# A two-level Strassen MLP on one core: product 6 of the second matmul also gets an inner level

## The chip, the cores and the metric

One core of a Trainium2 chip runs the kernel. The metric is the device time of one execution in microseconds (us); of a kernel that was run several times, the median is given. The engines of the core are TensorE (PE in the profile; its weight loads are PEld), VectorE (DVE), ScalarE (ACT), GpSimd (POOL) and SyncE (SP), which issues nearly all transfers.

## The reference

`x` is 1 x 2048 x 1024, `w1` 1024 x 3584, `w2` 3584 x 1024, all bf16.

```python
def reference(x, w1, b1, w2, b2):
    y = _layernorm(x, axis=-1)
    h = _gelu(jnp.einsum("bsd,df->bsf", y, w1) + b1)
    return jnp.einsum("bsf,fd->bsd", h, w2) + b2
```

## The kernel before

**Blocks.** The 2048 rows are two blocks (`s` = 0 and 1) of 1024. Each block runs matmul 1 (`y` times `w1`, then gelu into `h_sb`) and matmul 2 (`h` times `w2`). Both use Strassen's scheme in Winograd's form: an operand is cut into 2 x 2 quarters, seven products of quarter sums replace eight, and sums of the products give the four result quarters. The sums of operands are made by VectorE; those of `w2` are made once, in block 0, and kept in DRAM (`w2_sums`; in the code `tq`, with T1 to T4).

**Matmul 1 of block 1** runs in seven chunks of two units each; a chunk takes 28 x 2 matmuls of 512 columns on L608. Of product `P` in unit `u` the kernel keeps a copy `sn` (L621, ScalarE or VectorE), VectorE adds a later product to it (`c7`, `c3`, L626), and ScalarE applies gelu (L632). The next product in the same PSUM bank waits for the copy or the sum: P4 of a unit waits for its `c7`, P6 for the copy of P1, P7 for the copy of P6.

**Matmul 2** has seven products of 512 x 512 with a depth of 14 x 128. In block 1 they run in the order 1, 5, 2, 6, 7, 3, 4 (`SEQ2`). A product is run in one of two ways:

- `plain` (L797): four tiles, each of 14 matmuls of 512 columns; one operand is a whole quarter of `w2` (1792 KB).
- `inner` (L864): one more Winograd level. Seven sub-products, in the order 1, 5, 6, 2, 7, 3, 4, each of 14 matmuls of 256 columns. VectorE makes four sums of the `h` operand (`iS5`, `iS6`, `iS7`, `iS3`, each of 1792 16-bit columns, L681). Each sub-product has its own piece of `w2` of 448 KB: three raw, four sums that lie in DRAM (`w2_inner_sums`, `ti`). Sums of the sub-products follow on VectorE (L761) and ScalarE (L781): here called `k1`, `k2`, `k5` (intermediate), `o11`, `o12`, `o21`, `o22` (the four results) and `s2` (a copy into a bank that is accumulated upon).

`INNER` lists which products are `inner`; in block 1 all but product 6.

**Sums over products in block 1** (U and V style, in f32 tiles `sn_sb`): g1 is product 1, g5 product 5. Product 6 was accumulated by TensorE on top of g1: ScalarE first copies g1's four tiles into four banks (`seed`), the plain product is run on them, ScalarE copies the result out (`V`), and VectorE adds g5 (`O12`, four operations of 512 columns). Product 7 accumulates on V, product 3 on O12; `o22` adds g5 to product 7's result in four operations of 512 columns and is stored.

**The inner sums of w2.** Block 0 stores those of products 1 to 4 (`is`). For products 5 and 7 `t_inner` (L1130 and on) makes them during matmul 1 of block 1: SP loads one quarter from `w2_sums` into `x_sb` (`tl`, 1792 KB), VectorE makes four sums (`tI`, 1792 columns, L1138), and SP stores each (`ts`, 448 KB). The buffers are used in turn, so the load for product 7 waits until all four stores of product 5 have landed.

**What sets the order.** A planner (`Planner.place`) orders all operations of an engine before the kernel is built, by costs, due times and free buffers that are written into the code. Each engine then runs its list strictly in that order (`_emit`), with semaphore waits. So an operation that waits holds back everything behind it in its engine's list; SP's list of transfers is such a list too. TensorE has 8 PSUM banks; `sn_sb` has 12 tiles.

**Weights in block 1 of matmul 2** lie in 22 buffers of 448 KB (`A0`.. to `X1`); `hold` names, product by product, the buffers of its seven pieces. `fetch` issues their loads, each waiting for the sub-product that last read the buffer. Product 6, being plain, took the four buffers `A` at once (`load_w2`).

Of the kernel before, what the change touches and what calls it, by code (L numbers as in the profile page):

```python
# [29 lines left out]
N_WARM = 26  # L30
OPEN_JOBS = 5
SEQ2 = ((5, 1, 2, 6, 7, 3, 4), (1, 5, 2, 6, 7, 3, 4))
INNER = ((1, 2, 3, 4), (1, 5, 2, 7, 3, 4))
LN_ACT = (2, 4, 6)
DMA_T = (4, 6)

# [200 lines left out]
def bass_standalone__mixer_channel_mlp__prompt_kernel(  # L237
# [24 lines left out]
    with ExitStack() as es:  # L262
# [487 lines left out]
        def mm2_block(s, W):  # L750
# [6 lines left out]
            A = {q: (h[q], [[h_ok[(s, q, u)]] for u in range(NU)]) for q in h}  # L757
            users = {p: [] for p in SEQ2[s]}
            stores = []
            done = lambda p: users[p]  # L760
            plus = lambda e, out, x, y: e.tensor_tensor(out=out, in0=x, in1=y, op=ALU.add)  # L761

# [72 lines left out]
                users[p] += flat(t1, t2, t3, t4)  # L835
                return {1: Y["11"], 2: Y["21"], 3: Y["22"], 4: t4, 5: t1, 6: t2, 7: t3}

            def inner(p, a, Yo, xb, war, O=None, bias=None, out=None, gate=(), kk=None):

# [55 lines left out]

                g, ok = O
                ho = [Holder(outs, 2), Holder(outs, 2)] if out is not None else [None, None]
                hk = Holder(snaps) if kk is None else None  # L900

                def kk_q():
                    t = kk if hk is None else sn_sb[:, hk.k, :]
                    return t.rearrange("p (v c) -> p v c", v=2)

                def o_q(i, j):
                    return quart(g, i, j) if out is None else o_sb[:, ho[i].k:ho[i].k + 2, j * HI:(j + 1) * HI]

                sd = copy(lambda: bank_q(c2), lambda: quart(g, 0, 0), (ok[11], subs[1]), at[1], f"s2_{nm}", alloc=c2)
                k1 = copy(kk_q, lambda: bank_q(c0), (subs[1], *gate), end(1), f"k1_{nm}", alloc=hk)  # L910
                k5 = dve(lambda e: plus(e, quart(g, 1, 1), bank_q(c5), quart(g, 1, 1)), (subs[5], ok[22]), end(5), f"k5_{nm}")
                sub(6, (k1,))
                k2 = dve(lambda e: plus(e, quart(g, 0, 1), bank_q(c0), quart(g, 0, 1)), (subs[6], ok[12]), end(6), f"k2_{nm}")
                sub(2, (sd,))
                o11 = dve(lambda e: plus(e, o_q(0, 0), bank_q(c2), kk_q()), (subs[2], k1, sd), end(2), f"o11_{nm}",
                          alloc=ho[0], frees=(c2,) if hk is None else (c2, hk))
                sub(7, (k2,))
                o22 = dve(lambda e: plus(e, o_q(1, 1), bank_q(c0), quart(g, 1, 1)), (subs[7], k5), end(7), f"o22_{nm}",
                          alloc=ho[1])
                sub(3, (k5,))  # L920
                o12 = dve(lambda e: plus(e, o_q(0, 1), bank_q(c5), quart(g, 0, 1)), (subs[3], k2, o11), end(3), f"o12_{nm}",
                          frees=(c5,))
                if out is not None:
                    store(out, 0, 2, ho[0], (o11, o12), end(3))
                sub(4, (o22,))
                o21 = dve(lambda e: plus(e, o_q(1, 0), bank_q(c0), quart(g, 1, 0)), (subs[4], ok[21], o12, o22), end(4),
                          f"o21_{nm}", frees=(c0, g) if out is not None else (c0,))
                if out is not None:
                    store(out, 2, 2, ho[1], (o22, o21), end(4))
                users[p] += list(subs.values()) + flat(s1, s2, s3, s4)  # L930
                if out is None:
                    return g, {11: o11, 12: o12, 21: o21, 22: o22}, subs
                return subs
# [12 lines left out]
            def last_block():  # L946
# [39 lines left out]
                def give(names, subs):  # L986
                    for r, b in zip(SEQ1, names):
                        use[b] = [subs[r]]

                hold = {1: ("A0", "A1", "A2", "A3", "B0", "B1", "B2"), 5: ("V0", "V1", "Y0", "Y1", "Y2", "Y3", "Y4"),  # L990
                        2: ("W0", "W1", "Y5", "Y6", "Y7", "X0", "X1"), 7: ("B0", "B1", "B2", "B3", "V0", "V1", "Y0"),
                        3: ("Y1", "Y2", "Y3", "Y4", "W0", "W1", "Y5"), 4: ("Y6", "Y7", "X0", "X1", "A0", "A1", "A2")}
                Yo = {1: fetch(1, hold[1], base1[s] + 0.5 * T_MM1), 5: fetch(5, hold[5], pt[1] - 10),
                      2: fetch(2, hold[2], pt[1])}
                ring_of = lambda m: [*w1_use[m], *(o for l in t1_use[m].values() for o in l)]
                warX = {("S", r): ring_of(n - 1) + (ring_of(n) if r in (7, 3) else []) for r in (5, 6, 7, 3)}
# [7 lines left out]
                g5, ok5, sub5 = inner(5, S1, Yo[5], XT, warX, gate=(sub1[6],), bias=(  # L1004
                    dl_sb[:, None, 0:HI].to_broadcast([P, 2, HI]), e1_sb[:, None, :].to_broadcast([P, 2, HI])))
                give(hold[5], sub5)
                B6 = load_w2(s, "A", "T2", [o for k in range(4) for o in use[f"A{k}"]], pt[5])
                Yo[7] = fetch(7, hold[7], pt[2])
                hb = [Holder(banks, seeded=True) for _ in range(TH)]
                sdb = seed(1, hb, lambda t: tile_of(g1, t), [(ok1[11], ok1[12]) if t < 2 else (ok1[21], ok1[22])  # L1010
                                                             for t in range(TH)], pt[2])
                S2 = sums(h[11], S1, A[11], ALU.subtract, done(1), pt[5] + 2, f"hS2_{s}", step=(2, 4, 4, 4))
                S3 = sums(h[21], A[22], S2, ALU.subtract, done(5), pt[2] + 4, f"hS3_{s}", step=(4, 4, 4, 2))

                okw = {11: ok1[11], 12: sdb[1], 21: sdb[3], 22: sdb[3]}
                sub2 = inner(2, A[12], Yo[2], XX, war_of(sub1), O=(g1, okw), out=11, gate=W["x"])
                give(hold[2], sub2)
                S4 = sums(h[12], A[12], S2, ALU.subtract, done(2), pt[6], f"hS4_{s}", step=(4, 4, 4, 2))
                Yo[3] = fetch(3, hold[3], pt[6])

                M6 = plain(6, S2, B6, hb, False, [(o,) for o in sdb])
                g12, gv = Holder(snaps, 4), Holder(snaps, 4)
                O12, V = [], []
                for t in range(TH):
                    at = pt[6] + (t + 1) * SLOT2
                    ok_t = (ok5[11], ok5[12]) if t < 2 else (ok5[21], ok5[22])
                    V.append(copy(lambda t=t: tile_of(gv, t), lambda t=t: bank_t(hb[t]), (M6[t], *V[:1]), at, f"V_{s}_{t}",
                                  alloc=gv if t == 0 else None))
                    O12.append(dve(lambda e, t=t: plus(e, tile_of(g12, t), bank_t(hb[t]), tile_of(g5, t)),
                                   (M6[t], V[t], *ok_t, *O12[:1]), at, f"O12_{s}_{t}", alloc=g12 if t == 0 else None,  # L1030
                                   frees=(hb[t],)))
                for k in range(4):
                    use[f"A{k}"] = list(M6)
                Yo[4] = fetch(4, hold[4], pt[7])

                okv = {11: V[1], 12: V[1], 21: V[3], 22: V[3]}
                gw, okq, sub7 = inner(7, S3, Yo[7], XT, war_of(sub5), O=(gv, okv), kk=dl_sb[:, :], gate=(sub5[5],))
                give(hold[7], sub7)
                for i in range(2):
                    ho = Holder(outs, 2)  # L1040
                    f = []
                    for j in (1, 0):
                        q = 10 * (i + 1) + j + 1
                        f.append(dve(lambda e, i=i, j=j, ho=ho: plus(
                            e, o_sb[:, ho.k:ho.k + 2, j * HI:(j + 1) * HI], quart(gw, i, j), quart(g5, i, j)),
                            (okq[q], O12[3], *f), pt[7] + 7 * SUB + 0.1 * i, f"o22_{s}_{i}{j}",
                            alloc=ho if not f else None, frees=(g5,) if i and not j else ()))
                    store(22, 2 * i, 2, ho, f, pt[7] + 7 * SUB)

                sub3 = inner(3, S4, Yo[3], XX, war_of(sub2),  # L1050
                             O=(g12, {11: O12[1], 12: O12[1], 21: O12[3], 22: O12[3]}), out=12)
                inner(4, A[22], Yo[4], XT, war_of(sub7), O=(gw, okq), out=21,
                      gate=(f[-1],))

            def war_of(subs, p=None):
                return {(c, r): [subs[r]] + ([ti_st[p][r]] if c == "T" and r in ti_st.get(p, {}) else [])
# [116 lines left out]
        for s in range(NSB):  # L1173
            last = []
            for c in range(NC):
                n = s * NC + c
                t0 = base1[s] + c * 14 * SLOT
                if n:
                    T = w1_sums(s, c, t0 - 2 * SLOT)
                    for v in range(2):  # L1180
                        last += mm1_unit(s, c, v, T, t0 + v * SLOT)
                m = n + N_W1
                if m < (s + 1) * NC:
                    load_w1(s, m % NC, t0 + 14 * SLOT)
                if s == 0 and c == 1:
                    gate = (w1_use[0][-1],)
                    t11 = load_w2(0, "B", "B11", gate, t0 + 0.1)
                    t1q = w2_prep(t11[1][0][0], gate, t0 + 8, 8.5)
            if s == 0:
                W = {5: t1q, 1: t11, "C": last}  # L1190
            else:
                x_end = [o for i in range(NT) for o in x_free[(s, i)]] + wfree["outs"]
                e5 = t_inner(5, 0, x_end, base1[s] + 0.15 * T_MM1)
                e7 = t_inner(7, 2, e5, base1[s] + 0.4 * T_MM1)
                W = {"A": wfree["A"], "B": wfree["B"], "x": e7, "C": last}
            wfree = wf = mm2_block(s, W)
            if s + 1 < NSB:
                for c in range(N_W1):
                    load_w1(s + 1, c, base2[s] + 40 + c)
                for i in range(NT):  # L1200
                    load_x(s + 1, i, [*x_gate[i]], base2[s] - 4 + i)
                    ln_act2(s + 1, i, base2[s] + 10 + 5 * i, wf["ring"])
                    dma_T(s + 1, i, base2[s] + 30 + 3 * i, ((*last, *(wf["C"] if i >= TH else ())), last))
                y_sums(s + 1, base1[s + 1] - 14, wf["C"])
# [59 lines left out]
```

## Time and profile before

| | |
|---|---|
| median of 7 runs | 344.4 us (343.91 to 345.11) |
| the profiled execution's own time | 345.01 us |
| its span, first to last instruction | 343.3 us |
| granted TensorE clock, mean | 1.000 |
| TensorE busy | 335.6 us (98%), 2263 matmuls |
| VectorE busy | 259.3 us (76%), 363 instructions |
| ScalarE busy | 184.4 us (54%), 306 instructions |
| DMA, hardware queue q1 | 85.48 MB, 77.2% of 16 engines' span |
| matmul 1 of block 1, from its first unmixed stretch | 184 to 263.4 us |
| matmul 2 of block 1 | 263.4 to 339.8 us |
| one matmul of 512 columns there (12.09 us for 56) | 0.2159 us |
| one sub-product of 14 matmuls of 256 columns | 1.529 us |

The page gives busy times over the whole span. The windows view gives them for one stretch; the timeline lists instructions of one engine in order of time, merged where they are alike, with the idle time before them in brackets and what ended it. The chain of waits follows the last instruction back to whatever released it. TensorE's records overlap, so the step from one start to the next is the cost of a matmul, not its own duration of 379 or 273 ns.

### The profile page before, as it was taken

To read this page: it belongs to the slowest core of one execution; us is meant where nothing else is said; L and a number is where in the kernel's file an instruction comes from. 1 tells how busy PE (TensorE), PEld (TensorE's weight loads), DVE (VectorE), ACT (ScalarE), POOL (GpSimd) and SP (SyncE) were. 2 spreads that over 40 slices of the span, in tenths; PEclk is the share of its full clock that TensorE was granted. 3 is DMA by queue.
4 is the path that set the end of the run, shared out by engine and by line. 5 is a ranking of instruction groups with operands and counts; after the bars stand their busy time and mean duration, and the time that the engine had idled before them with its cause. 6 is when DMAs were issued, how large, how long until landed. Compare 5 with 4: busy or idle time off the path is not lost.

```text
span 343.3 us, 5750 instructions
## 1 busy us (share of the span) xinstructions
PE 335.6 (98%) x2263; PEld 210.9 (61%) x2263; DVE 259.3 (76%) x363; ACT 184.4 (54%) x306; POOL 23.5 (7%) x47
## 2 busy tenths in 40 slices
PE   5999999999999999999999999999999999999995
PEld 4977444444444885547875444444445888658885
DVE  4779988989657599859999579596338968798733
ACT  4674666766788878732113776667676441021110
POOL 2320000000003223320000000000000000000000
PEclk9999999999999999999999999999999999999999
DMA  7748999997969999599799998992133999964111
GB/s 233 258 83 285 352 356 326 286 336 253 362 218 325 284 331 207 110 271 383 254 333 321 337 315 264 351 277 59 68 107 95 357 381 362 343 196 156 63 61 63
DMA packets 75141, 85.98 MB, mean 250 GB/s; under 512 B 13930, under 2 KB 63082, under 8 KB 74346
## 3 DMA queue, kind: packets, MB, share of 16 engines
q1 hardware_dynamic: 74970, 85.48, 77.2%
q8 instruction: 18, 0.29, 0.3%
q10 hardware_dynamic: 144, 0.13, 0.1%
q14 instruction: 9, 0.07, 0.1%
HBM read 60.43 MB, written 22.54 MB: 242 GB/s over the span
## 4 chain that ended last, share of the span: by engine, by line
PE 97%; DMA 2%; SPq 0%; DVE 0%; issue 0%
PE ps L608 46%; PE ps L864 31%; PE ps L797 14%; PE ps L566 5%; DMA w_sb<-in_w_dram 2%; PE ps L472 1%; SPq L327 0%; DVE o_sb L761 0%; PE ps L383 0%
## 5 line engine op out<-in xcount | busy, mean ns | idle before, releaser
L608 PE MATMUL ps<-yw_sb,t_sb 128*128 128x512 f16 x416 | 96.1, 379 | 0.0
L608 PE MATMUL ps<-yw_sb,w_sb 128*128 128x512 f16 x312 | 73.7, 379 | 0.0
L608 PEld LDWEIGHTS ps<-yw_sb,t_sb 128*128 128x128 f16 x416 | 40.6, 98 | 48.7
L608 PEld LDWEIGHTS ps<-yw_sb,w_sb 128*128 128x128 bf16 x312 | 30.4, 98 | 36.2 <-ACT ps L621 0.3
L626 DVE TENSOR_TENSOR sn_sb<-ps,sn_sb 128x512 f32<-128x512 f32 x54 | 36.3, 687 | 18.6 <-PE ps L608 18.2
L797 PE MATMUL ps<-w2a_sb,h_sb 128*128 128x512 f16 x224 | 49.3, 379 | 0.0
L632 ACT ACTIVATE h_sb<-sn_sb,b_sb 128x512 f16<-128x512 f32 x54 | 38.2, 718 | 17.0 <-DVE sn_sb L626 15.0
L681 DVE TENSOR_TENSOR h_sb<-h_sb 128x1024 f16<-128x1024 f16 (+2 forms) x42 | 38.6, 950 | 2.9 <-ACT h_sb L632 2.1
L632 ACT ACTIVATE h_sb<-ps,b_sb 128x512 f16<-128x512 f32 x50 | 34.1, 685 | 11.2 <-PE ps L608 10.6
L621 ACT COPY sn_sb<-ps 128x512 f32<-128x512 f32 x50 | 29.3, 586 | 20.0 <-PE ps L608 19.9
L797 PEld LDWEIGHTS ps<-w2a_sb,h_sb 128*128 128x128 f16 x224 | 21.9, 98 | 25.4
L781 ACT COPY sn_sb<-ps 128x512 f32<-128x512 f32 x30 | 17.3, 581 | 33.0 <-PE ps L797 19.4
L761 DVE TENSOR_TENSOR o_sb<-ps,sn_sb 128x512 bf16<-128x512 f32 x28 | 19.1, 687 | 13.5 <-PE ps L864 12.0
L761 DVE TENSOR_TENSOR sn_sb<-ps,sn_sb 128x512 f32<-128x512 f32 x31 | 21.3, 686 | 9.7 <-PE ps L864 9.0
L781 ACT COPY ps<-sn_sb 128x512 f32<-128x512 f32 x15 | 8.8, 589 | 34.3 <-PE ps L864 30.5
L864 PE MATMUL ps<-w2a_sb,h_sb 128*128 128x256 f16 (+1 forms) x196 | 23.5, 273 | 0.0
L864 PE MATMUL ps<-w_sb,t_sb 128*128 128x256 f16 x182 | 21.7, 273 | 0.0
L541 DVE TENSOR_TENSOR t_sb<-w_sb,t_sb 128x1024 f16<-128x1024 bf16 x26 | 17.9, 687 | 4.6 <-PE ps L608 3.9
L864 PEld LDWEIGHTS ps<-w2a_sb,h_sb 128*128 128x128 f16 x196 | 19.2, 98 | 3.3
L864 PEld LDWEIGHTS ps<-w_sb,t_sb 128*128 128x128 f16 x182 | 17.8, 98 | 2.3
L541 DVE TENSOR_TENSOR t_sb<-w_sb 128x1024 f16<-128x1024 bf16 x26 | 17.7, 682 | 0.3 <-PE ps L608 0.2
L566 PE MATMUL ps<-yw_sb,w_sb 128*128 128x128 f16 x256 | 17.0, 231 | 0.3 <-DMA w_sb<-in_w_dram 0.3
(91 smaller groups left out, 374.5 us busy)
## 6 DMA issues: line engine op xcount, KB each, us to landing
w_sb<-in_w_dram SPq DMA_DIRECT2D x28, 512.0 KB, 6.4
x_sb<-in_w_dram SPq DMA_DIRECT2D x21, 256.0 KB, 4.9
w_sums<-x_sb SPq DMA_DIRECT2D x21, 256.0 KB, 5.4
w_inner_sums<-w_sb SPq DMA_DIRECT2D x12, 448.0 KB, 5.3
w2a_sb<-w_sums SPq DMA_DIRECT2D x3, 1792.0 KB, 9.1
yw_sb<-w_inner_sums SPq DMA_DIRECT2D x10, 448.0 KB, 8.0
x_sb<-in_x_dram SPq DMA_DIRECT2D x15, 256.0 KB, 6.4
w2a_sb<-in_w_dram SPq DMA_DIRECT2D x2, 1792.0 KB, 9.6
```

The lines of the kernel that those rows point to most:

```text
L472: fn = [(lambda e, j=j, k=k, hold=hold: e.transpose(out=ps16[:, hold.k, j * P:(j + 1) * P], in_=x16[:, i, k * HT + j * P:k * HT + (j + 1) ...
L541: return add("DVE", 0.65, lambda e: e.tensor_tensor(out=tv(k), in0=x0, in1=x1, op=ALU.subtract), [*deps, *war.get(k, ())], prio + 0.5 * k, ...
L566: fn = [(lambda e, b=b, hb=hold[f], f=f, k=k, t=t: e.matmul(ps[:, hb.k, t * P:(t + 1) * P], lhsT=lhs[:, k, f * P:(f + 1) * P], rhs=yop[f"A ...
L608: fn = [(lambda e, k=k: e.matmul(ps[:, hold[p].k, :], lhsT=lhs[:, k, :], rhs=yop[yo][:, k, :], start=(first and k == 0), stop=(k == KH - 1 ...
L621: return e.copy(out=dst, in_=src) if o_.eng == "ACT" else e.tensor_copy(dst, src)
L626: return add("DVE", 0.69, lambda e: e.tensor_tensor(out=sn_sb[:, hold_s.k, :], in0=ps[:, hold[p].k, :], in1=sn_sb[:, hold_s.k, :], op=ALU. ...
L632: r = h_ok[(s, q, u)] = add("ACT", 0.70, lambda e: e.activation(out=h[q][:, u, :], in_=src(), func=ACT.Gelu_apprx_tanh, bias=b1_sb[:, f:f ...
L681: o = add("DVE", cost2(w * dst.shape[-1]), lambda e, k0=k0, k1=k1: e.tensor_tensor(out=dst[:, k0:k1, :], in0=a[0][:, k0:k1, :], in1=b[0][: ...
L761: plus = lambda e, out, x, y: e.tensor_tensor(out=out, in0=x, in1=y, op=ALU.add)
L781: return act(lambda e: e.copy(out=out(), in_=src()), deps, at, name, **k)
L797: fn = [(lambda e, k=k, t=t: e.matmul(ps[:, banks_[t].k, :], lhsT=a[0][:, k, t * P:(t + 1) * P], rhs=b[0][:, k, :], start=(first and k == ...
L864: fn = [(lambda e, k=k, j=j: e.matmul(ps[:, bank[r].k, j * HI:(j + 1) * HI], lhsT=x[0][:, k, j * P:(j + 1) * P], rhs=y[0][:, k, :], start= ...
```

## The change

Product 6 of block 1 becomes `inner`. Its 56 matmuls of 512 columns become 98 of 256. A third `t_inner`, between those of products 5 and 7, makes its `w2` sums, and seven pieces of 448 KB take the place of its one load of 1792 KB (`hold` is dealt anew). Product 2, which used to overwrite g1 while it was summed, now writes into four fresh tiles (`tmp`), so that g1 stays whole and product 6 accumulates onto it in f32 on VectorE; the four seeding copies and the four copies `V` go. `O12` and the sums `o22` are each made in two operations of 1024 columns instead of four of 512. Product 7's `h` sums go to `x_sb` instead of `t1_sb`, those of products 3 and 4 the other way round.

```diff
-INNER = ((1, 2, 3, 4), (1, 5, 2, 7, 3, 4))
+INNER = ((1, 2, 3, 4), (1, 5, 2, 6, 7, 3, 4))
...
+                gt = g if tmp is None else tmp
...
-                k5 = dve(lambda e: plus(e, quart(g, 1, 1), bank_q(c5), quart(g, 1, 1)), (subs[5], ok[22]), end(5), f"k5_{nm}")
+                k5 = dve(lambda e: plus(e, quart(gt, 1, 1), bank_q(c5), quart(g, 1, 1)), (subs[5], ok[22], k1), end(5), f"k5_{nm}")
...
-                Yo = {1: fetch(1, hold[1], base1[s] + 0.5 * T_MM1), 5: fetch(5, hold[5], pt[1] - 10),
+                Yo = {1: fetch(1, hold[1], base1[s] + 0.6 * T_MM1), 5: fetch(5, hold[5], pt[1] - 10),
...
-                B6 = load_w2(s, "A", "T2", [o for k in range(4) for o in use[f"A{k}"]], pt[5])
+                Yo[6] = fetch(6, hold[6], pt[5])
                 Yo[7] = fetch(7, hold[7], pt[2])
-                hb = [Holder(banks, seeded=True) for _ in range(TH)]
-                sdb = seed(1, hb, lambda t: tile_of(g1, t), [(ok1[11], ok1[12]) if t < 2 else (ok1[21], ok1[22])
-                                                             for t in range(TH)], pt[2])
...
-                sub2 = inner(2, A[12], Yo[2], XX, war_of(sub1), O=(g1, okw), out=11, gate=W["x"])
+                sub2 = inner(2, A[12], Yo[2], XX, war_of(sub1), O=(g1, ok1), out=11, gate=W["x"], tmp=Holder(snaps, 4))
...
-                M6 = plain(6, S2, B6, hb, False, [(o,) for o in sdb])
-                g12, gv = Holder(snaps, 4), Holder(snaps, 4)
-                O12, V = [], []
-                for t in range(TH):
-                    at = pt[6] + (t + 1) * SLOT2
-                    ok_t = (ok5[11], ok5[12]) if t < 2 else (ok5[21], ok5[22])
-                    V.append(copy(lambda t=t: tile_of(gv, t), lambda t=t: bank_t(hb[t]), (M6[t], *V[:1]), at, f"V_{s}_{t}",
-                                  alloc=gv if t == 0 else None))
-                    O12.append(dve(lambda e, t=t: plus(e, tile_of(g12, t), bank_t(hb[t]), tile_of(g5, t)),
...
+                _, okv, sub6 = inner(6, S2, Yo[6], XT, war_of(sub5), O=(g1, {q: last_[q] for q in ok1}))
+                give(hold[6], sub6)
+                g12 = Holder(snaps, 4)
+                O12 = {}
+                for i in range(2):
+                    q = 10 * i + 11
+                    rows = lambda g, i=i: sn_sb[:, g.k + 2 * i:g.k + 2 * i + 2, :]
+                    O12[q] = O12[q + 1] = add("DVE", 1.22, lambda e, rows=rows: plus(e, rows(g12), rows(g1), rows(g5)), (
+                        okv[q], okv[q + 1], ok5[q], ok5[q + 1], *O12.values()), pt[7] + 0.1 * i, f"O12_{s}_{i}",
+                        alloc=None if O12 else g12)
...
-                gw, okq, sub7 = inner(7, S3, Yo[7], XT, war_of(sub5), O=(gv, okv), kk=dl_sb[:, :], gate=(sub5[5],))
+                gw, okq, sub7 = inner(7, S3, Yo[7], XX, war_of(sub2), O=(g1, O12), kk=dl_sb[:, :], gate=(sub5[5],))
...
+                    f = [add("DVE", 1.22, lambda e, i=i, ho=ho, rows=rows: plus(
+                        e, o_sb[:, ho.k:ho.k + 2, :].rearrange("p v (j c) -> p v j c", j=2), rows(gw), rows(g5)),
+                        (okq[q], okq[q + 1], *O12.values()), pt[7] + 7 * SUB + 0.1 * i, f"o22_{s}_{i}", alloc=ho,
+                        frees=(g5,) if i else ())]
...
-                e5 = t_inner(5, 0, x_end, base1[s] + 0.15 * T_MM1)
-                e7 = t_inner(7, 2, e5, base1[s] + 0.4 * T_MM1)
+                e5 = t_inner(5, 0, x_end, base1[s] + 0.14 * T_MM1)
+                e6 = t_inner(6, 1, e5, base1[s] + 0.32 * T_MM1)
+                e7 = t_inner(7, 2, e6, base1[s] + 0.5 * T_MM1)
```

The order of instructions that the planner now writes differs in these places of block 1:

- SP: `tl6` stands where `tl7` stood; four stores `ts6` follow, `tl7` comes after the loads of the last chunk of `w1`, and the seven loads for product 6 stand where its one load stood.
- VectorE, matmul 1: `c3` of unit 3 is moved in front of the last sum for product 5; the four `tI6` stand between `hS1_2` (a sum of `h` for product 5) and `c7` of unit 6; the four `tI7` between `w1T3` of chunk 6 and `c3` of units 8 and 9. Behind these stand copies of units 11 and 10 (`sn5`, `sn6`) that VectorE takes over from ScalarE.
- TensorE, matmul 2: products are interleaved by sub-products. In sub-products counted from the start of matmul 2 (number 0 is sub-product 1 of product 1), numbers 0 to 19 are products 1 and 5 and the first six of product 2, as before; then come 6.1, 2.4, 6.5, 6.2, 6.6, 7.1, 7.5, 6.7, 6.3, 7.6, 6.4, 7.2, 7.7, 3.1, 7.3, 7.4, 3.5, 3.2, 4.1, 3.6, 3.3, 3.7, 4.5, 3.4, 4.6, 4.2, 4.7, 4.3, 4.4 (product.sub-product), the last being number 48.
- VectorE, matmul 2: `iS5`, `iS6`, `iS7` of product 6 stand among the sums of product 5's results, `iS3` of product 6 behind `k2` of product 2; the sums of product 6 and the two `O12` stand among the `h` sums for product 3 and the sums of product 7.

## Prediction

> **What bounds the kernel now.** I read the page's chain of waits first, then the same chain in order of time, then the windows of matmul 2 of block 1, product by product, then the timelines.
>
> The page says who sets the end:
>
> ```profile
> PE 97%; DMA 2%; SPq 0%; DVE 0%; issue 0%
> ```
>
> In order of time, the last part of the chain (start us, us, what) has TensorE without a gap from 263.51 to 339.80; after it come one sum and the last store:
>
> ```profile
> 263.51 30.57 PE ps L864 x280
> 294.08 3.02 PE ps L797 x14
> 297.10 1.53 PE ps L864 x14
> 298.63 9.07 PE ps L797 x42
> 307.69 32.11 PE ps L864 x294
> 339.80 0.02 issue
> 339.83 0.69 DVE o_sb L761
> ```
>
> So any TensorE time saved ends the run earlier, one for one, and any stall of TensorE is paid one for one. L797 is product 6, in 3.02 + 9.07 us; L864 is all else. Below (window, length, then busy us of PE, PEld, DVE, ACT, POOL, clock, DMA share, GB/s) are products 1, 2, 6 and 7:
>
> ```profile
> 263.35:274.05 10.70, 10.70 (x100) 9.59 (x98) 9.96 (x12) 5.60 (x11) 0.00 (x0) 1.00 1.03 335
> 284.75:293.92 9.17, 9.17 (x87) 8.22 (x85) 8.50 (x10) 1.70 (x3) 0.00 (x0) 1.00 1.09 354
> 293.92:307.53 13.61, 13.61 (x72) 6.85 (x70) 11.42 (x14) 1.76 (x3) 0.00 (x0) 1.00 0.87 281
> 307.53:318.20 10.67, 10.67 (x99) 9.56 (x98) 9.07 (x12) 1.69 (x3) 0.00 (x0) 1.00 0.42 131
> ```
>
> The reader is to see TensorE full at clock 1.00, VectorE 80 to 93% busy, and the DMA engines saturated up to about 300 us. The second and third may become late.
>
> **What TensorE gains.** Removed: 56 matmuls of 512 columns, 12.09 us by the chain. Added: 7 sub-products of 14 matmuls of 256. The piece of 280 such matmuls takes 30.57 us, so 14 take 1.529 us and seven 10.70. Gain: 12.09 - 10.70 = **1.39 us**. The weight loads double per column, yet stages with only 256-column matmuls run at half the price per matmul (0.1092 against 0.2159 us) with PEld at 9.59 of 10.70 us, so nothing hidden there shows.
>
> A rule of the Trainium skill speaks against the change: "TensorE: Matmul & The Clock Gate", section "Back-to-back issue gap", gives about 131 ns per matmul of 512 columns and 81 ns of 128 in a sustained stream. On the line between these, 256 columns would cost an estimated 98 ns, and the change would lose 98 x 0.098 - 56 x 0.131 = 2.3 us. This trace has 216 and 109 ns, so the measurement decides; the isolated formula of that section, N/2.4 + 2.5, fits both.
>
> **VectorE in matmul 2.** Removed: four `O12` and four `o22` of 0.69, 5.5 us. Added: four sums of 1792 columns (1.08), six sums out of PSUM (0.69), four operations of 1024 f32 columns. The last form is not in the trace. Below it lies one sum of 512 f32 columns, 0.69; above it two of these, 1.38. The 16-bit rows (1024 columns 0.69, 1792 1.08, 2048 1.22) rise by 0.53 us per 1024, and 512 f32 cost what 1024 16-bit do; so I take the 2048 row, 1.22. Sum: 4.3 + 4.1 + 4.9 - 5.5 = +7.8 us. By the windows from 263.35 to 340 VectorE was busy for 57.6 of 76.6 us, now 65.4 of 75.2: it fits on average, and what counts is each sum that TensorE waits for. ScalarE loses eight copies and gains two here; it is idle most of the time.
>
> I walked VectorE's new list by hand. Sub-product number k starts at 263.36 + 1.529 k, and its result can be read 1.73 us after (263.35 to 265.08 for the first). Steps in a full queue are 1.00 for 1792 columns, 1.14 for 2048, 0.60 for a sum out of PSUM, 0.10 to 0.12 more where an operation needs the one before it:
>
> - The two sums of product 5, 281.91 and 283.44, come on time. `iS7` of product 6 makes the `h` sums for product 7 start at 285.04 instead of 284.95. `k2` of product 2 runs at 289.66 (289.56 before), done 290.35; its reader starts at 290.88: slack 0.5.
> - `o21` of product 2 starts at 297.74 behind `iS3` of product 7; the four sums of 2048 and 1024 fill it to 302.36. Then `k5` and `k2` of product 6, done 303.65; sub-product 6.7 starts at 304.64: slack 0.9.
> - **Tightest:** 6.3 (number 28) can be read at 307.90; `o12` of product 6 to 308.59; `O12` 308.63 to 309.85; ScalarE's `s2` for product 7, 309.94 to 310.53; sub-product 7.2 (number 31) starts at 310.76. Slack 0.2, with its weight load inside.
> - `o22` ends at 321.56, ScalarE's `k1` of product 3 waits for the buffer this frees, 322.2; 3.6 starts at 322.99: slack 0.8. Behind that, 0.6 and more.
>
> A hand-over between dependent sums costs little (VectorE timeline; the second needs the first):
>
> ```profile
> 315.37 0.69 DVE L761 TENSOR_TENSOR sn_sb<-ps,sn_sb 128x512 f32<-128x512 f32 x1 [0.70 <-PE ps L864]
> 316.10 0.69 DVE L761 TENSOR_TENSOR o_sb<-sn_sb 128x512 bf16<-128x512 f32 x1
> ```
>
> I cost this part at 0 to 0.2 us, and take 0.05.
>
> **Transfers in matmul 2.** Seven pieces (3.21 MB) replace 1.84 MB, +1.38 MB. At 360 GB/s a piece takes 1.27 us, less than the 1.529 us in which a sub-product uses one up. The eight loads ahead are issued by about 272 us as before; the pieces of product 6 follow 1.3 us apart and, at about 8 us to landing, are there from 280 to 289. They are needed from 293.9 to 309.2. Those of product 7, from 289 to 296, are needed from 303. Cost 0, with some 13 us of cover; the waits for free buffers all end before. The new sources are in 512-byte runs, as three pieces of every product already are.
>
> **Matmul 1 of block 1: the risk.** Here +1.84 MB load, +1.84 MB stores, four more sums (4.4 us) on VectorE and four more copies (2.4 us). VectorE was busy for 8.1, 8.2, 11.0, 6.9 and 4.8 us of the 12.09 us chunks from 196 on, so there is room. But VectorE waits for the load in its list. The timeline:
>
> ```profile
> 216.68 0.68 DVE L681 TENSOR_TENSOR h_sb<-h_sb 128x1024 f16<-128x1024 f16 x1
> 220.27 2.09 DVE L1138 TENSOR_TENSOR o_sb<-x_sb 128x1792 f16<-128x1792 f16 x2 [2.91 <-DMA x_sb<-w_sums]
> 222.39 1.09 DVE L1138 TENSOR_TENSOR x_sb<-x_sb,o_sb 128x1792 f16<-128x1792 f16 x1
> 223.40 1.28 DVE L626 TENSOR_TENSOR sn_sb<-ps,sn_sb 128x512 f32<-128x512 f32 x2
> 224.60 1.08 DVE L1138 TENSOR_TENSOR x_sb<-x_sb 128x1792 f16<-128x1792 f16 x1
> ```
>
> It shows VectorE held for 2.91 us by the load `tl7` (issued 212.96, landed 7.3 us later). Two `c7` sums then ran ahead of the last `tI`. Now `tl6` is in that place and all four `tI6` come first: the last at 223.50, `c7` of unit 6 at 224.50 to 225.19. P4 of unit 6 starts at 225.36. Slack 0.1 with a weight load in it: 0 to 0.2 us lost, I take 0.1.
>
> `tl7` is issued when the last `ts6` has landed: stored at 224.7, 6.2 us (as before, 206.72 to 212.96) give 230.9; landed 7.3 us later, 238.2. VectorE reaches `tI7` at 237.1, so it waits for 1.1 us. Four sums take 4.2, `c3`, `c3` and `sn5` 1.8, `sn6` of unit 10 0.7: done 244.9. P7 of unit 10 starts at 246.08, its weight load a little before: slack 1.0. Its `ts7`, landing at 248.8, hold `iS7` of product 1 by some 0.2 us; the next reader has 1 us. Cost 0. Without this cover each us of delay is 1 us of time.
>
> SP's list moves nothing else: behind `tl7` wait loads that were not issued before 237.64 anyway, when their buffers come free.
>
> **Sum.** -1.39 + 0.10 + 0.05, about -1.25 us: the profiled execution's 345.01 (1.7 us outside its span) would be 343.8. It lies 0.6 above the median, 344.4, from which the forecast for a median is **343.15**.
>
> **Rivals.**
>
> 1. *The sums or hand-overs in products 6 and 7 are later than my walk* (or small losses add up). For: three slacks of 0.5 or less. Against: the steps are measured in this trace, and `O12` cannot exceed 1.38. If three places lose 0.2 to 0.4 each beyond the slack, 0.7 to 1.2 us of 1.39 go: 343.9 to 344.2, within 0.2%. A measurement of this kernel can't tell less than 0.2% (0.7 us) from no change.
> 2. *Slower: the loads `tl6` or `tl7` land late* and VectorE, held by them, is late with `c7` of unit 6 or `sn6` of unit 10. For: the load of product 5 took 9.9 us (issued 191.25, its reader at 201.17). At 9.9 instead of 7.3, `tl6` costs 2.6 us beyond a slack of almost nothing: 343.15 + 2.6 = 345.75. `tl7` at 9.9 would cost 1.6 more, as its slack is 1.0. It decides from a landing of 8.6 us for `tl6`. Against: `tl6` has the very place of a load that took 7.3, and `tl7` runs when only 78 GB/s were moved (windows, 232.27 to 244.36).
> 3. *It doesn't do what it says*: 256-column matmuls that don't halve. 98 of them and 56 of 512 stand in the same trace with the prices above; the only way left is a lower clock under denser weight loads, and stages of that density have 1.00. Two per cent less over 49 sub-products would cost 1.5 us and take the gain; its chance is counted with rival 2.
>
> **How the numbers follow.** Forecast 0.64 (own range 342.6 to 343.6), rival 1 0.21, rivals 2 and 3 0.15. The range must reach past rival 1's times and leave 0.15 out above: 342.6 to 344.6. Faster by over 0.2% (under 343.7) 0.64, same 0.21, slower (over 345.1) 0.15.
>
> **What would show it.** Right: the piece of the chain from matmul 2's start to its end is 74.9 us instead of 76.3, all L864; VectorE's wait for `w_sums` stands once at about 220 and once for about 1 us before 238.5; 1024-column sums take 1.22. Wrong: an idle stretch of PE or PEld with VectorE as its releaser near 225.3, 246, 310.7 or 323, or L626 as an idle time of ACT in 238 to 248; a PE piece of 14 matmuls longer than 1.53.

## The result, and the profile after

The changed kernel takes **343.68 us** (median of 26 runs, 342.40 to 345.29), the kernel before, run beside it, 344.95 (68 runs): ratio 0.9963, 95% interval 0.9954 to 0.9973, or 0.9 to 1.6 us less. The forecast was 343.15 with a change of -1.25 us; the medians differ by -1.27, and that these two agree to 0.02 us is luck within such an interval. The forecast's level is half a us low because the first seven runs of the kernel before were: their median was 344.40, that of all 68 is 344.95.

(In the changed kernel's lines L866 stands for what was L864, L798 for L797, L762 for L761, L782 for L781 and L1136 for L1138.) The last part of the chain of waits in the profile of the changed kernel, in order of time (start us, us, what):

```profile
184.11 79.43 PE ps L608 x368
263.54 74.90 PE ps L866 x686
338.44 0.02 issue
338.47 0.69 DVE o_sb L762
```

From 184.11 to 338.44 there is nothing but matmuls: matmul 1 of block 1 in 79.43 us, then matmul 2 in one piece of 74.90, 686 matmuls, all of one line. In the kernel before matmul 2 was 263.51 to 339.80, 76.29 us, and matmul 1 ahead of it took as long as now:

```profile
184.09 79.43 PE ps L608 x368
```

The difference in matmul 2, 1.39, is the whole change between the two profiles from 184 us on; no part of it was lost in stalls. The table of TensorE's waits has three entries, of 1.0, 2.9 and 0.3 us, all in the first 9 us of the run.

The windows of sub-products 26 to 32 (four of product 7 and the last three of product 6) and of what follows them (window, length, then busy us of PE, PEld, DVE, ACT and POOL, clock, DMA share, GB/s):

```profile
303.10:313.80 10.70, 10.70 (x100) 9.58 (x99) 9.63 (x12) 1.18 (x2) 0.00 (x0) 1.00 1.07 353
313.80:326.00 12.20, 12.20 (x114) 10.92 (x113) 11.61 (x15) 2.28 (x4) 0.00 (x0) 1.00 0.15 52
```

TensorE is full at clock 1.00 and VectorE is 90 and 95% busy. In the window before these, 293.92 to 303.10, with four of product 6's seven sub-products, it is 98% busy, and PEld 8.24 of 9.18 us, the same share as in the other inner products. Over all of matmul 2 VectorE is busy for 64.4 of 75.2 us; the prediction had 65.4.

The tightest point, product 6's last sum ahead of product 7. VectorE, then ScalarE, then TensorE (timelines of the changed kernel):

```profile
307.90 0.69 DVE L762 TENSOR_TENSOR sn_sb<-ps,sn_sb 128x512 f32<-128x512 f32 x1 [0.84 <-PE ps L866]
308.62 1.22 DVE L762 TENSOR_TENSOR sn_sb<-sn_sb 128x1024 f32<-128x1024 f32 x1
...
309.88 0.59 ACT L782 COPY ps<-sn_sb 128x512 f32<-128x512 f32 x1 [5.98 <-DVE sn_sb L762]
...
310.75 1.69 PE L866 MATMUL ps<-yw_sb,h_sb 128*128 128x256 f16 x14
```

The joined sum of 1024 columns takes 1.22 us, as taken from the 16-bit row. The copy ends at 310.47, and sub-product 7.2 starts at 310.75 without a wait.

VectorE's sums of the loads for products 6 and 7 in matmul 1 (timeline):

```profile
220.00 2.09 DVE L1136 TENSOR_TENSOR o_sb<-x_sb 128x1792 f16<-128x1792 f16 x2 [2.62 <-DMA x_sb<-w_sums]
...
237.16 2.09 DVE L1136 TENSOR_TENSOR o_sb<-x_sb 128x1792 f16<-128x1792 f16 x2
```

It waits for the first load as before (2.62 us; 2.91 before), and not at all for the second. There the prediction had a wait of 1.1 us. The list of SP shows why: the second load is issued at 228.62, not at the predicted 230.9. The table of transfers (window 220 to 240) gives its time to landing in the last column.

```profile
221.12 1.34 SPq L327 DMA_DIRECT2D w_inner_sums<-o_sb  x2
223.25 1.64 SPq L327 DMA_DIRECT2D w_inner_sums<-x_sb  x2
...
228.62 0.34 SPq L327 DMA_DIRECT2D x_sb<-w_sums  x1
```

```profile
x_sb<-w_sums SPq DMA_DIRECT2D x1, 1792.0 KB, 8.2
```

The issue of the last of the four stores begins at 224.38, and the load goes out 4.2 us later; in the kernel before 6.2 us lay between the same two (206.74 to 212.96). The load itself took longer than the 7.3 us of the prediction: it landed 8.2 us after its issue, at 236.8, only some 0.3 us before VectorE came to it at 237.16.

### The profile page after: what moved, and what is told of

Same layout as the page of the kernel before. It is cut to its first block, busy times and chain, and to the rows that moved or that the text cites. A ratio compares the mean times of both kernels' runs of the same rounds, so it can differ in the third digit from the quotient of the medians.

```text
span 342.0 us, 5853 instructions
## 1 busy us (share of the span) xinstructions
PE 334.2 (98%) x2305; PEld 215.1 (63%) x2305; DVE 272.8 (80%) x377; ACT 178.9 (52%) x296; POOL 23.5 (7%) x47
## 4 chain that ended last, share of the span: by engine, by line
PE 97%; DMA 1%; DVE 1%; ACT 0%; POOL 0%; issue 0%
PE ps L608 46%; PE ps L866 34%; PE ps L798 11%; PE ps L566 5%; PE ps L472 1%; DMA x_sb<-in_x_dram 1%; DVE st_sb L395 0%; DVE o_sb L762 0%; ACT yw_sb L479 0%; POOL rstd_sb L402 0%; DVE x_sb L405 0%; DVE mv_sb L398 0%; DVE vpe_sb L399 0%; PE ps L383 0%
## 5 line engine op out<-in xcount | busy, mean ns | idle before, releaser
L626 DVE TENSOR_TENSOR sn_sb<-ps,sn_sb 128x512 f32<-128x512 f32 x54 | 36.1, 686 | 15.1 <-PE ps L608 14.8
L621 ACT COPY sn_sb<-ps 128x512 f32<-128x512 f32 x46 | 26.9, 586 | 20.2 <-PE ps L608 19.9
L798 PE MATMUL ps<-w2a_sb,h_sb 128*128 128x512 f16 x168 | 36.9, 379 | 0.0
L782 ACT COPY sn_sb<-ps 128x512 f32<-128x512 f32 x27 | 15.6, 581 | 27.2 <-DVE o_sb L762 13.2
L866 PE MATMUL ps<-w2a_sb,h_sb 128*128 128x256 f16 (+1 forms) x238 | 28.6, 273 | 0.0
L798 PEld LDWEIGHTS ps<-w2a_sb,h_sb 128*128 128x128 f16 x168 | 16.4, 98 | 19.2
L762 DVE TENSOR_TENSOR sn_sb<-ps,sn_sb 128x512 f32<-128x512 f32 x33 | 22.4, 685 | 5.8 <-PE ps L866 5.3
L762 DVE TENSOR_TENSOR o_sb<-ps,sn_sb 128x512 bf16<-128x512 f32 x28 | 19.1, 687 | 9.7 <-PE ps L866 8.1
L866 PEld LDWEIGHTS ps<-w2a_sb,h_sb 128*128 128x128 f16 x238 | 23.3, 98 | 3.5
L782 ACT COPY ps<-sn_sb 128x512 f32<-128x512 f32 x12 | 7.1, 588 | 30.9 <-PE ps L866 24.4
L866 PE MATMUL ps<-w_sb,t_sb 128*128 128x256 f16 x168 | 20.1, 273 | 0.0
L866 PEld LDWEIGHTS ps<-w_sb,t_sb 128*128 128x128 f16 x168 | 16.4, 98 | 2.1
L566 PE MATMUL ps<-yw_sb,w_sb 128*128 128x128 f16 x256 | 17.0, 232 | 0.3 <-ACT yw_sb L479 0.3
```

The lines of the kernel that those rows point to most:

```text
L566: fn = [(lambda e, b=b, hb=hold[f], f=f, k=k, t=t: e.matmul(ps[:, hb.k, t * P:(t + 1) * P], lhsT=lhs[:, k, f * P:(f + 1) * P], rhs=yop[f"A ...
L621: return e.copy(out=dst, in_=src) if o_.eng == "ACT" else e.tensor_copy(dst, src)
L626: return add("DVE", 0.69, lambda e: e.tensor_tensor(out=sn_sb[:, hold_s.k, :], in0=ps[:, hold[p].k, :], in1=sn_sb[:, hold_s.k, :], op=ALU. ...
L782: return act(lambda e: e.copy(out=out(), in_=src()), deps, at, name, **k)
L798: fn = [(lambda e, k=k, t=t: e.matmul(ps[:, banks_[t].k, :], lhsT=a[0][:, k, t * P:(t + 1) * P], rhs=b[0][:, k, :], start=(first and k == ...
L866: fn = [(lambda e, k=k, j=j: e.matmul(ps[:, bank[r].k, j * HI:(j + 1) * HI], lhsT=x[0][:, k, j * P:(j + 1) * P], rhs=y[0][:, k, :], start= ...
```

## The experiments

My theory: TensorE sets the end from 184 us on, the change is worth the 1.39 us that its matmuls take less, and all it adds elsewhere is covered, by little at two hand-overs (0.2 us at 7.2, 0.1 us at P4 of unit 6) and by more at a third (P7 of unit 10). Rivals: a part of the gain is lost somewhere that no gap shows (copies, transfers, the wide operations); or the covers are much larger or smaller than walked, and the outcome was luck. So one run undoes a part, three push a hand-over out of its cover, one takes the added work out of matmul 1. The last few are about the spread between executions. Each group shares its runs of the kernel before.

**The base of the first group.**

> The changed kernel as it is, as the base of this set. Expected: TensorE runs without a gap from about 29.95 to 338.4 us, matmul 2 of block 1 takes 74.9 us, time about 1.3 us (0.37%) under the kernel before on the same chip.

Measured: 343.47 us (12 runs), kernel before 344.96 (35 runs), ratio 0.9959, interval 0.9940 to 0.9978. In its profile, too, matmul 2 is one piece of 74.90 us.

**The wide sums in halves again**, those of `O12` as below and those of `o22` likewise.

```diff
-    O12[q] = O12[q + 1] = add("DVE", 1.22, ... plus(e, rows(g12), rows(g1), rows(g5)), ...)
+    for j in range(2):
+        q = 10 * i + 11 + j
...
+        O12[q] = dve(... plus(e, row(g12), row(g1), row(g5)), ...)
```

> The changed kernel, but O12 and o22 each in four operations of 512 columns instead of two of 1024; product 6 keeps its inner level. Theory (the gain is TensorE's 12.09 - 10.70 us, and VectorE has cover): VectorE is busy for 4 x 0.16 = 0.6 us more and TensorE still has no gap, so the time is that of the changed kernel within 0.2 us. Rival (the joined sums carry part of the gain): 0.5 us or more is lost against the changed kernel, and TensorE waits for VectorE near 310 to 323 us.

Measured: 343.74 us (12 runs), ratio 0.9962, interval 0.9942 to 0.9982, against 0.9959 for the base; in its profile matmul 2 is one piece of 74.90 us. Joining the sums is worth nothing that can be measured here. It does make the hand-over tight: in this run the first half of `O12` needs only `o11` of product 6's sums and starts at 304.74, ScalarE's copy ends at 306.06, and 7.2 starts at 311.23, so the copy is 5 us ahead of it, where the joined sum, which needs `o12` too, leaves 0.3. But TensorE was not waiting in either.

**One more wide sum ahead of O12**, only before the first (`i` = 0), into a free output buffer (the edit in outline).

```diff
     for i in range(2):
+        plus(e, o_sb[:, hx.k:hx.k + 2, :], rows(g1), rows(g5))
         O12[q] = O12[q + 1] = add("DVE", 1.22, ...)
```

> The changed kernel with one more VectorE operation of 1024 f32 columns ahead of the first O12 (its result, in spare columns of o_sb, is used by nobody). VectorE's step is 1.14 us. Theory: the slack of the chain o12 of product 6, O12, s2 of product 7, sub-product 7.2 is 0.2 us, so TensorE stalls for 0.9 to 1.0 us at 310.7 us and nowhere else for more than 0.3, and the time rises by 0.9 to 1.2 us over the changed kernel. Rival (the order has cover there of a us or more): no gap, same time as the changed kernel.

Measured: 344.39 us (10 runs), ratio 0.9997, interval 0.9975 to 1.0019; 0.92 us above the base. VectorE, ScalarE and TensorE at the hand-over in its profile (this execution runs 1.16 us ahead of the one shown above):

```profile
307.45 1.23 DVE L762 TENSOR_TENSOR o_sb<-sn_sb 128x1024 bf16<-128x1024 f32 x1
...
308.06 1.69 PE L866 MATMUL ps<-w2a_sb,h_sb 128*128 128x256 f16 x14
308.60 1.22 DVE L762 TENSOR_TENSOR sn_sb<-sn_sb 128x1024 f32<-128x1024 f32 x1
309.85 0.59 ACT L782 COPY ps<-sn_sb 128x512 f32<-128x512 f32 x1 [7.12 <-DVE sn_sb L762]
...
310.49 1.70 PE L866 MATMUL ps<-yw_sb,h_sb 128*128 128x256 f16 x14 [0.74 <-ACT ps L782]
```

Sub-product 6.4, which runs just ahead of 7.2, starts at 308.06, so 7.2 was due 1.53 later, at 309.59; it starts at 310.49, 0.90 late, and the releaser is ScalarE's copy. `O12` is 1.14 us later than in the changed kernel (308.60 + 1.16 against 308.62). So the cover was 1.14 - 0.90 = 0.24 us, with 0.2 predicted. One operation more of 1.2 us in this place takes back most of the gain.

**The load for product 6 later.**

```diff
     order = pl.place()
+    named["tl6"].deps.append(named["P4_1_5"])
```

> The changed kernel, but the load tl6 is issued only when P4 of unit 5 is done, about 215.2 instead of 212.8 us; all orders are kept. Theory: VectorE is held by it until about 222.4 instead of 220.0, c7 of unit 6 is done at about 227.4, P4 of unit 6 was due at 225.4 with some 0.35 us of cover, so TensorE stalls for about 2.1 us there (1.7 to 2.6) and the time is 0.6 to 1.2 us above the kernel before. Rival (the five open units cover it): TensorE loses under 0.5 us.

Measured: 346.26 us (10 runs), ratio 1.0036, interval 1.0016 to 1.0056: 2.8 us above the base by the medians, and slower than the kernel before. VectorE and TensorE in its profile:

```profile
223.29 2.09 DVE L1136 TENSOR_TENSOR o_sb<-x_sb 128x1792 f16<-128x1792 f16 x2 [4.82 <-DMA x_sb<-w_sums]
...
227.55 2.48 DVE L626 TENSOR_TENSOR sn_sb<-ps,sn_sb 128x512 f32<-128x512 f32 x4
```

```profile
224.75 1.89 PE L608 MATMUL ps<-yw_sb,w_sb 128*128 128x512 f16 x8
228.29 1.90 PE L608 MATMUL ps<-yw_sb,t_sb 128*128 128x512 f16 x8 [1.66 <-DVE sn_sb L626]
```

P4 of unit 6 was due 8 x 0.216 = 1.73 us after 224.75 and starts 1.8 us late, with `c7` (L626) as its releaser. This is the mechanism of the prediction's rival 2, with its price. Counted from the start of the stretch, `c7` starts 2.19 us later than in the changed kernel (227.55 - 185.20 against 224.27 - 184.11) and 1.81 of these were lost, so 0.38 us had been covered, more than the 0.1 of the prediction. The profile shows 1.8 us of the 2.8, and its span is 1.9 longer than that of the base (344.9 against 343.0). The medians' other 0.9 us, which put them 1.3 above the kernel before where I had allowed 0.6 to 1.2, has no place in these two traces. Four of the ten executions have a mean clock of 0.99, as one of the base's twelve has; without these the medians are still 2.6 apart (345.99 and 343.41), so the cause of the rest stays open.

**The load for product 7 later.** The edit is the same with `tl7` and `P2_1_8`.

> The changed kernel, whose load `tl7` waits in addition for P2 of unit 8, so it is issued at about 233.4 us of the span instead of 228.6. It tests the slack that the prediction gave the hand-over from the second load to `sn6` of unit 10. My theory: the load lands 6.3 to 7.4 us later, at 239.7 to 240.8, so VectorE is held from 237.2 for 2.5 to 3.6 us; the first 2.0 us of this are covered (without a hold `sn6` of unit 10 is done at about 244.4, and P7 of unit 10 starts at 246.1 with its weight load a little before), so TensorE loses 0.4 to 1.5 us ahead of P7 of unit 10 and the median lies 0.4 to 1.5 us above the changed kernel's of the same call. Rival: the hold is paid from its start, 2.5 to 3.6 us above the changed kernel. Third way: nothing is lost, because other waits were shorter than I think; then TensorE has no gap near 246.

> The changed kernel again, as the base of this call: as before, about 1.3 us below the kernel before (343.4 to 343.7 us), with the stretch of matmul 2 of block 1 at 74.90 us.

Measured, in one group: 344.54 us (12 runs; ratio 1.0005, interval 0.9990 to 1.0020) against 343.07 for the changed kernel (11 runs; 0.9961, 0.9946 to 0.9976). The difference is 1.47 us. The chain in order of time of the delayed kernel, then VectorE and TensorE at the hand-over:

```profile
182.81 49.22 PE ps L608 x228
...
232.12 7.46 DMA x_sb<-w_sums
...
239.60 2.10 DVE o_sb L1136 x2
...
246.40 17.44 PE ps L608 x80
263.84 74.90 PE ps L866 x686
```

```profile
239.60 2.09 DVE L1136 TENSOR_TENSOR o_sb<-x_sb 128x1792 f16<-128x1792 f16 x2 [3.66 <-DMA x_sb<-w_sums]
246.40 1.90 PE L608 MATMUL ps<-yw_sb,t_sb 128*128 128x512 f16 x8 [1.42 <-DVE sn_sb L621]
```

Now the load stands in the chain, and P7 of unit 10 waits for the copy behind it. The stretch from 182.81 to 263.84 is 81.03 us long, 1.60 more than the 79.43 of the changed kernel. VectorE was held for 3.66 us, so 2.06 were covered: 2.0 had been worked out. The rival, paid from the start, is out.

**Matmul 1 without the added work**; `pi` is 5 where `p` is 6, so product 6 is computed with product 5's inner sums.

```diff
-    e6 = t_inner(6, 1, e5, base1[s] + 0.32 * T_MM1)
-    e7 = t_inner(7, 2, e6, base1[s] + 0.5 * T_MM1)
+    e7 = t_inner(7, 2, e5, base1[s] + 0.5 * T_MM1)
...
-    o = dma(d, ti[p - 1, j - 1], [*use[b], *ti_ok[(p, j)]], ...)
+    o = dma(d, ti[pi - 1, j - 1], [*use[b], *ti_ok[(pi, j)]], ...)
```

> The changed kernel without the inner sums of product 6's weights in matmul 1 (the load `tl6`, four sums on VectorE, four stores; `tl7` is issued in the place of `tl6`): product 6 fetches the four inner sums of product 5 instead, so the output is not the reference's and all of matmul 2 costs what it did. It takes away everything that the change added to matmul 1 of block 1. My theory: this part is covered in full, since the profile of the changed kernel has no gap of TensorE there; the median is that of the changed kernel, within 0.3 us. Rival: the added transfers and sums cost something that the gaps do not show (a slower matmul while copies and transfers share the memory, say); then it is more than 0.5 us faster, and the stretch of chain over matmul 1 (79.43 us in the changed kernel) is shorter by as much.

Measured: 343.57 us (12 runs), ratio 0.9967, interval 0.9953 to 0.9981, against 343.07 and 0.9961 for the changed kernel of the same group. Not faster, so the rival is out. The 0.5 us above the base is more than the 0.3 I allowed, but the intervals overlap almost wholly and the chain has the same two stretches, 79.42 and 74.90 us. 1.84 MB of loads, as much of stores and 4.4 us of VectorE cost matmul 1 nothing: 79.42 us without them, 79.43 with them.

**The start of the run.** The stretches above agree to 0.01 us between executions in which nothing is late, yet in the four profiles of the changed kernel the stretch begins at 184.11, 185.09, 183.75 and 184.26. So the spread of the changed kernel arises ahead of that. In the base of the first group TensorE had the granted clock 0.50 from about 8 to 14 us, in the other three 1.00. (The medians of the two later bases, 343.07 and 343.86, lie on either side of the 343.1 to 343.7 expected of them.) One line was changed, `N_WARM`, the number of idle matmuls at the start, from 26 to 56 and to 36.

> The changed kernel with 56 instead of 26 idle matmuls of 128 columns ahead of the first transposes (nothing else). It is about the spread between executions and not about the change: in two of the four profiles of the first call TensorE worked only 0.62 us and then waited 1.2 to 1.45 us for ScalarE's copy at about 7 to 8.5 us, and the granted clock was 0.50 from 8.2 to about 14 us, which cost 1 us; in the others (1.03 us of work, gap 0.34 to 0.64) it stayed 1.00. Theory: it is the low activity before 8 us that lowers the clock; with the idle matmuls running to about 6 us instead of 4.0 the clock stays 1.00 in every profile, and the median falls by 0.2 to 0.7 us, with fewer executions above 344. Rival: it is the gap after the transposes alone; then the profile can show 0.50 again, and the median is that of the changed kernel, within 0.2.

> The changed kernel with 36 instead of 26 idle matmuls at the start. In the profile with 56 of them, they ran at about 90 to 100 ns each up to about 4.4 us and at about 40 ns from 5 us on, and every later matmul of 128 columns ran at about 60 ns; with 26, which end at 4.0 us, the matmuls of the first tiles ran at 116 ns up to 10 to 14 us. Theory: what counts is that TensorE works without a pause for some 3.4 us from its start; 36 end at about 4.8 us, so the full rate is there too, and the median is that of the kernel with 56, 0.4 to 1.0 us below the changed kernel. Rival: the pause that follows (4.8 to 6.4 us) takes the rate back; then the first tiles run at 116 ns again and the median is that of the changed kernel, within 0.2.

> The kernel with 56 idle matmuls again, for more executions: 0.7 us below the changed kernel, as in its first call (342.37 against 343.07), and 1.9 to 2.2 us below the kernel before. If the 0.7 was chance among six executions, it is within 0.2 of the changed kernel.

> The changed kernel as the base of this call: 343.1 to 343.7 us, 1.3 below the kernel before.

Measured: with 56 idle matmuls 342.37 us (6 runs; ratio 0.9944, interval 0.9926 to 0.9961) against 343.07 in its group, and again 342.48 (6 runs; 0.9928, 0.9911 to 0.9945) against 343.86 (0.9971, 0.9955 to 0.9986): 0.7 and 1.4 us less than the changed kernel, the second twice what was expected. With 36: 343.20 (12 runs; 0.9954, 0.9937 to 0.9972). TensorE at the start, in the changed kernel (base of the third group):

```profile
1.04 2.95 PE L377 MATMUL ps<-ones 128*128 128x128 f16 x26 [1.04 <-POOL ones L352]
6.65 1.03 PE L472 MATMUL ps<-ident,x_sb 128*128 128x128 f16 x8 [2.65 <-DVE x_sb L405]
8.38 1.86 PE L566 MATMUL ps<-yw_sb,w_sb 128*128 128x128 f16 x16 [0.70 <-ACT yw_sb L479]
10.04 1.06 PE L472 MATMUL ps<-ident,x_sb 128*128 128x128 f16 x8
```

with 56 (third group):

```profile
1.04 4.70 PE L377 MATMUL ps<-ones 128*128 128x128 f16 x56 [1.04 <-POOL ones L352]
6.74 0.62 PE L472 MATMUL ps<-ident,x_sb 128*128 128x128 f16 x8 [0.99 <-DVE x_sb L405]
8.66 1.05 PE L566 MATMUL ps<-yw_sb,w_sb 128*128 128x128 f16 x16 [1.31 <-ACT yw_sb L479]
9.55 0.61 PE L472 MATMUL ps<-ident,x_sb 128*128 128x128 f16 x8
```

and with 36:

```profile
1.04 3.83 PE L377 MATMUL ps<-ones 128*128 128x128 f16 x36 [1.04 <-POOL ones L352]
6.58 0.62 PE L472 MATMUL ps<-ident,x_sb 128*128 128x128 f16 x8 [1.70 <-DVE x_sb L405]
8.51 1.86 PE L566 MATMUL ps<-yw_sb,w_sb 128*128 128x128 f16 x16 [1.31 <-ACT yw_sb L479]
10.17 1.06 PE L472 MATMUL ps<-ident,x_sb 128*128 128x128 f16 x8
```

From the start of L566 to the next line, 16 matmuls take 1.66 us in the first (104 ns each) and 0.89 in the second (56 ns): half rate and full rate. With 36 idle matmuls (3.83 us, to 4.87) the transposes (L472) start after a pause of 1.70 us and take 0.62 us as with 56, but L566 starts at 8.51, after a pause of 1.31, and the next line 1.66 us later: half rate again. My theory for 36, that reaching the full rate once is enough, fell: its expected rival, that the pauses take the rate back, is what the profile shows. The rival for 56, that the pause after the transposes lowers the rate, fell too: the second fence has that pause, 1.31 us, and the full rate. What differs is the pause of 1.70 against 0.99 us ahead of the transposes, or the longer work before it; these runs don't separate the two (36 was profiled once, 56 twice). In two executions with 26 (the base of the first group and the delayed `tl6`) the transposes took 0.62 us too, after pauses of 2.63 and 2.50 us, and L566 was at half rate behind them as with 36. The time with 36 is between the other two and tells nothing.

The kernel with 56 is the fastest of all: 2.2 us and 2.5 us below the kernel before in its two groups.

## Why the prediction was right

- *TensorE's gain, 1.39 us.* Right as it stands: 76.29 - 74.90 in the two profiles. The prices of 0.1092 us per matmul of 256 columns and 0.2159 of 512 held in the new place. The estimate from the Trainium skill, "TensorE: Matmul & The Clock Gate", section "Back-to-back issue gap", a loss of 2.3 us, is contradicted by these runs.
- *Product 6's sums.* The walk was right to a few hundredths: `O12` at 308.62 (walked 308.63) for 1.22 us, the copy at 309.88 (309.94), sub-product 7.2 at 310.75 (310.76). The slack of 0.2 measured 0.24 by the added sum. The 0.05 us that I charged for this part was not lost.
- *Matmul 1, first load.* The load took the place of the one for product 7, VectorE's sums began at 220.00, and `c7` of unit 6 came in time. The 0.10 us charged here was not lost either: the cover was nearer 0.4 us than 0.1. That it is thin all the same is shown by the delayed load, which costs 1.8 us of TensorE's time in the profile.
- *Matmul 1, second load.* The mis-sized term. I took 6.2 us from the last store to the next load, as in the kernel before; it was 4.2. The landing was mis-sized the other way, 8.2 us for 7.3. With the last store issued 0.3 us earlier than forecast, the load landed at 236.8 instead of 238.2, so the wait of 1.1 us did not occur, by 0.3 us. It did not matter, since this hand-over has 2.1 us of cover (1.1 of wait and 1.0 of slack in the prediction's terms, the same sum).
- *Transfers in matmul 2 at nothing.* Right: with the DMA engines saturated there (345 to 359 GB/s in the page's slices from 265 to 308 us), no matmul waited. The first piece of product 6 was issued at 272.11 and landed 7.9 us later, 14 us before its sub-product starts at 293.94, as the 13 us of the prediction have it.
- *Rival 1* (lost in the sums) failed by little: 0.24 us were left at one point. (Its price has a slip: three places at 0.2 to 0.4 us are 0.6 to 1.2, not 0.7 to 1.2.) *Rival 2* (a late load) has the mechanism and about the price that was given, and only its condition was not met. *Rival 3* is out: the clock was 1.00 in matmul 2 under the denser weight loads.

So the two small losses together, 0.15 us, were too many, and the change of the medians, -1.27 with 0.9 to 1.6 as its interval, can't tell -1.25 from -1.39; the profiles can. The path was right: TensorE sets the end, and what came off it came off the time.

## What to carry to other kernels

Where one engine works without a gap up to the end, a change is worth what it takes off that engine, provided that every hand-over on its way still comes in time: walk the feeding engine's list operation by operation, and name the smallest slack instead of the mean load (VectorE was up to 98% busy over a window and delayed nothing). A cover of 0.2 us holds as well as one of 13 until something is put in front of it; then each us is paid in full. And where executions spread by 2 us, look at the first 15 us for what the engine's rate does.

## What was not expected of the hardware

- The rate of TensorE's first matmuls depends on how it was kept busy before. At the start 26 idle matmuls take 2.95 us, 113 ns each; with 56, the rate rises in the course of them, and the tiles that follow run at 56 instead of 104 ns per matmul of 128 columns. With 56 the whole takes 0.7 to 1.4 us less. The Trainium skill, "TensorE: Matmul & The Clock Gate", "What's actually happening", has a clock that is halved until TensorE has been busy for about 3.4 us. These runs agree for the most part: after 2.95 us of idle matmuls the eight transposes took about 1.03 us in three of the four profiles of the changed kernel, and 0.62 in the fourth; after 4.70 and 5.11 us they took 0.62. They add that the rate can be lost soon: after 3.83 us of work it was gone behind pauses of 1.70 and 1.31 us around 0.62 us of work.
- The granted clock of the profile does not always show this: in the changed kernel's first profile the windows 8.20 to 12.00 and 12.00 to 16.00 us have a clock of 1.00 with 36 and 69 matmuls; in the base of the first group they have 0.50 and 0.70, with 34 and 54. So about as many matmuls run in the first window under 1.00 as under 0.50, and matmuls of 104 ns stand under a clock of 1.00.
- The same kind of store of 448 KB to DRAM, four in a row, was followed by the next load 4.2 us after the issue of the last in one place and 6.2 in another. The other traffic may be the reason; no run was made to separate it.
